# The first expert's low weight halves all on VectorE, its list joins and flags later, w_out's low products last

## The chip, the cores and the metric

The kernel runs on one core of one Trainium2 chip. The metric is the device time of one execution in microseconds (us), smaller being better. Beside the timed runs there is one profiled execution, from which the trace comes. Engines are called TensorE (PE in the rows), VectorE (DVE), ScalarE (ACT), GpSimd (POOL) and SyncE (SP, which here issues most of the DMA transfers); PEld is TensorE's weight load.

## The reference

Attention with a local band and a few global keys, then a dense feed-forward layer, then a top-1 mixture of eight experts. Cut to what matters:

```python
x = attention(q, k, v)                  # 2 x 8 heads x 768 x 64 -> x: 1536 x 512
h = x @ w_in                            # 512 x 2048
x = (h / (1 + exp(-h))) @ w_out         # 2048 x 512
logits = x @ w_gate                     # 512 x 8
e_idx = argmax(logits, axis=1)
gate_w = softmax(logits)[arange(N), e_idx]
eom = sigmoid(x @ w_output_gate)        # 512 x 8
for e in range(8):
    mask = e_idx == e
    ye = maximum(x[mask] @ w1[e], 0) @ w2[e]      # 512 x 1024, 1024 x 512
    out[mask] = gate_w[mask, None] * eom[mask, e, None] * ye
```

## The kernel before

**High and low halves.** A float32 product is made as three products of a rounded format (fp32r): every operand is split into a high half (a rounding copy) and a low half (the operand less its high half), and high x high, high x low and low x high are summed in PSUM. The high half is a copy on ScalarE, the low half a subtraction on VectorE or GpSimd that needs the high half first.

**Stages.** Attention runs over twelve blocks of 128 tokens. The feed-forward layer runs over five groups of 256-token pairs, the first of two pairs and the others of one (`CH`), and each group over 16 slices of the hidden dimension (`f`, called steps 0 to 15 here). In a step TensorE makes the 12 products of `w_in` for slice `f` (`s1_mm`, L315), ScalarE and VectorE evict them in four instructions (L319, L320, L323, L324), and TensorE makes the `w_out` products of slice `f-2` (`s2_mm`, L330 to L332): six per pair, for each of two 128-token halves high x high, low x high and high x low. `w_out`'s low halves are made during the first group and kept in DRAM (`wlo_d`); in later groups SyncE loads them again, four buffers (`wolr`). The evicted slices have six buffers (`g`).

**The first expert, early.** After the last but one group the most used expert so far is known (`order(0)`). In the last ten steps (6 to 15) of the last group, `moe2_pre(k)` loads that expert's weights as 16 quarters of 128 x 512 (`load_u`, SyncE, eight staging buffers `qr`) and splits them (`split_u`, L480 high on ScalarE, L481 low). Steps 8 to 15 split 2, 2, 2, 3, 3, 1, 1 and 2 quarters. In `split_u`, `pool=None` puts the low half of odd `i` on GpSimd and that of even `i` on VectorE. GpSimd also gathers the first rows of that expert (`early_load`, L494) and splits two of the three row blocks (L517). After the last `w_out` product the first 128 rows go through the first expert (`early1` to `early4`).

**The experts.** `order(1)` sorts the experts by use. `load_i(p)` loads two lists of places for expert p (L580), `min_i(p)` joins them by a minimum on VectorE (L584), and `load_x` gathers rows by the joined list (L587, GpSimd). `flags()` is eleven small VectorE instructions whose result is read once, after the last expert. The pass over expert p has eight steps `f`: `f1_mm` (w1 products), `f1_ev` (its eviction, two VectorE and two ScalarE instructions where the window is under 256 rows, as for the first expert), the splits of the next expert's quarters (0, 0, 3, 3, 3, 3, 2, 2 of them in steps 0 to 7; in each step one comes between the two halves of the eviction, and every fourth low half is GpSimd's), `prep_x` (transposes of the next expert's gathered rows) in one step per 128 rows, and `f2_mm` of two steps earlier. The w1 products alternate between two PSUM banks, so step 2 needs step 0's eviction.

**What sets the order.** The program is scheduled by hand: every engine runs its instructions in the order in which the code issues them. An instruction that waits holds up all that stands behind it on its engine, and so it is on SyncE's and GpSimd's DMA queues.

Of the kernel before, what the change touches and what calls it, by code (L numbers as in the profile page):

```python
# [10 lines left out]
F32 = mybir.dt.float32  # L11
# [8 lines left out]
P = 128  # L20
# [3 lines left out]
def kernel(ctx, tc, qk, v, n_global, n_local, w_in, w_out, wg, w1, w2, out):  # L24
# [3 lines left out]
    CH=[[0,1],[2],[3],[4],[5]]  # L28
# [35 lines left out]
    woh={}  # L64
# [256 lines left out]
    def s1_sp(u_,f):  # L321
        t=s1p.pop((u_,f)); g=mp.tile([P,2,256],F32R,tag="g",name="g",bufs=6); gg[u_,f]=g
        A.activation(out=g[:,0],in_=t,func=AF.Copy)  # L323
        V.tensor_tensor(out=g[:,1],in0=t,in1=g[:,0],op=ALU.subtract)  # L324
    def s2_mm(c,u,f):
        if f==0: s2p[u]=[ps.tile([P,512],F32,tag=f"s2{2*(u if c==0 else 0)+k}",name=f"s2{k}",bufs=1) for k in range(2)]
        g=gg.pop((u,f)); wl=wol[c,f]; wh=woh[f//2][:,f%2]
        for k in range(2):
            sl=slice(k*P,(k+1)*P)
            T.matmul(s2p[u][k],g[:,0,sl],wh,start=(f==0),stop=False)  # L330
            T.matmul(s2p[u][k],g[:,1,sl],wh,start=False,stop=False)  # L331
            T.matmul(s2p[u][k],g[:,0,sl],wl,start=False,stop=(f==FB-1))  # L332
    def s2_ev(u):
        xr=mp.tile([P,2,XW],F32,tag="stage",name="xr",bufs=2)
        for k in range(2):
# [236 lines left out]
    def tiles(p):  # L572

        return [(j,min(P,WIN[p]-j*P)) for j in range(R0[p]//P,(WIN[p]+P-1)//P)]
# [7 lines left out]
    def min_i(p):  # L582
        t=ixt[p]; nt=(WIN[p]+P-1)//P
        V.tensor_tensor(out=t[:,0,:nt],in0=t[:,0,:nt],in1=t[:,1,:nt],op=ALU.min)  # L584
# [55 lines left out]
    def moe2_pre(k):  # L640

        q=[(q,i) for q in (0,2,1,3) for i in range(KC)]
        w=(0,0,2,2,2,3,3,1,1,2)
        if 6<=k<16:
            for _ in range(w[k-6]): split_u(*q[nq[1]]); nq[1]+=1
            while nq[0]<min(16,nq[1]+4*(k-5),nq[1]+NQR): load_u(*q[nq[0]]); nq[0]+=1
        if k==6: early_iota()
        if k==7: early_load()
        if k==8: early_rows()
        if k==13: early_prep()  # L650
    def moe2():
        late_split()
        early1(0,0)
        run_gates(2)
        early1(0,1)
        logits(NTT-2)
        early1(1,0)
        run_gates(1)
        late1()
        run_gates(1)  # L660
        early1(1,1)
        early2(0)
        late3()
        order(1)
        moe2_open2()
        load_i(0); load_i(1)
        early3(0,0)
        early2(1)
        early3(0,1); min_i(0); min_i(1); early3(1,0)
        for p in (1,0):  # L670
            for j,n in tiles(p): load_x(p,j)
        early3(1,1)
        flags()
        early4()
        atags[0]=['a','pv','s23']
        LG=2
        steps=[(p,f) for p in range(NE) for f in range(8)]
        for g in range(len(steps)+LG):
            if g<len(steps):
                p,f=steps[g]  # L680
                def spl():
                    split_u(4*(p+1)+nq[1]//4,nq[1]%4,nq[1]%4==1); nq[1]+=1
                f1_mm(p,f)
                if p+1<NE and f==0: nq[:]=[0,0]
                ns=(0,0,3,3,3,3,2,2)[f] if p+1<NE else 0
                f1_ev(p,f,spl if ns else lambda: None)
                if p+1<NE:
                    for _ in range(ns-1): spl()
                    while nq[0]<min(16,nq[1]+4*(f+1),nq[1]+NQR): load_u(4*(p+1)+nq[0]//4,nq[0]%4); nq[0]+=1
                    if p and f==0:  # L690
                        for j,n in tiles(p+1): load_x(p+1,j)
                    if p==0 and f==5:
                        for j,n in tiles(0): fac_x(0,j)
                    if f==2 and p+2<NE: load_i(p+2)
                    if f==5 and p+2<NE: min_i(p+2)
                    t=tiles(p+1)
                    px=PX if p else 3
                    if px<=f<px+len(t): prep_x(p+1,t[f-px][0])
            if g>=LG:
                p2,f2=steps[g-LG]  # L700
                if p2<NE-1:
                    f2_mm(p2,f2)
                    if f2==7: f2_ev(p2)
                elif f2<LASTF:
                    f2_mm(p2,f2)
                elif f2==7:
                    for r in tiles(p2):
                        for k in range(LASTF,8): f2_mm(p2,k,[r])
                        f2_ev(p2,[r])
# [224 lines left out]
    with tc.manual_schedule():  # L934
# [23 lines left out]
        for g in range(len(steps)+LAG):  # L958
# [21 lines left out]
                if g>=LAG+FB: run_gates(2 if g==(len(CH)-1)*FB+2 else 1)  # L980
            if g>=LAG:
                c2,f2=steps[g-LAG]
                for u in CH[c2]:
                    s2_mm(c2,u,f2)
                if f2==FB-1:
                    for u in CH[c2]: gq.append(lambda u=u: s2_ev(u))
                    if c2==0: gq.append(lambda: atags.__setitem__(0,['a','s22','s23']))
                    for u in CH[c2]:
                        for n in (2*u,2*u+1): gq.append(lambda n=n: gate1(n))
                        for fn in (gate2,gate3): gq.append(lambda u=u,fn=fn: fn(u))  # L990
                    run_gates(3 if c2==0 else 1)
                    if c2==len(CH)-2: gq.append(lambda: order(0))
                    if c2==len(CH)-2: gq.append(moe2_open)
# [48 lines left out]
```

## Time and profile before

| | |
|---|---|
| median of 3 runs | 650.11 us (647.69 to 650.35) |
| the profiled execution | 648.54 us |
| its span | 646.8 us |
| TensorE busy | 597.0 us (92%) |
| VectorE busy | 387.3 us (60%) |
| ScalarE busy | 303.4 us (47%) |
| GpSimd busy | 218.0 us (34%) |
| TensorE, 1152 products of w_in (L315) | 154.6 us |
| VectorE, 81 low halves of expert weights (L481) | 75.4 us, 948 ns each on the mean |
| GpSimd, 31 such halves | 40.2 us, 1309 ns each |

Times in the trace count from the span's start. An engine that stands idle costs time only where the chain of work that ends last passes through it; in this kernel that chain lies on TensorE for 78% of the span. Products are pipelined, so a row's duration is longer than the distance to the next row, and the distance is what counts.

### The profile page before, as it was taken

The page shows a single profiled execution, that of the slowest core. Times are in us where ns is not written, and L with a number is a line of the kernel's source. Part 1 is how long each engine was busy: PE and PEld are TensorE (multiplying, and loading weights), DVE is VectorE, ACT ScalarE, POOL GpSimd, SP SyncE. Part 2 cuts the span into 40 slices and gives each one's busy share as a digit, 9 for nine tenths or more (in the row PEclk, how much of TensorE's full clock was granted, in tenths as well). Part 3 has the DMA queues.
Part 4 walks back from the last instruction along what each step waited for, and adds up shares of the span by engine and source line. Part 5 has one row for each costly group of instructions (what it writes and reads, how often), then busy time and mean ns, then how long its engine had stood idle before and what let it go on. Part 6 is the DMA issues. An engine that isn't in the chain of part 4 may idle for free.

```text
span 646.8 us, 12049 instructions
## 1 busy us (share of the span) xinstructions
PE 597.0 (92%) x4054; PEld 506.2 (78%) x4054; DVE 387.3 (60%) x1052; ACT 303.4 (47%) x802; POOL 218.0 (34%) x256
## 2 busy tenths in 40 slices
PE   1898999999997799999999999796999999999994
PEld 1566788888886678888889999685888888888783
DVE  3677589999453545645453344743845479778840
ACT  5577434344442334343432335441745556676741
POOL 3466524444231242222221002731452334443311
PEclk9999999999998999999999999798999999999998
DMA  7144607664347887396447349605957377577500
GB/s 252 41 131 149 225 6 221 221 220 136 121 106 78 131 159 181 98 154 163 124 95 135 83 86 248 201 20 118 295 184 217 111 265 232 185 245 262 171 17 19
DMA packets 83673, 98.77 MB, mean 153 GB/s; under 512 B 35547, under 2 KB 49883, under 8 KB 83602
## 3 DMA queue, kind: packets, MB, share of 16 engines
q1 hardware_dynamic: 76850, 86.69, 49.3%
q0 software_dynamic: 3312, 8.08, 3.8%
q10 hardware_dynamic: 3440, 3.15, 1.6%
q8 instruction: 34, 0.56, 0.4%
q14 instruction: 37, 0.30, 0.2%
HBM read 81.85 MB, written 11.52 MB: 144 GB/s over the span
## 4 chain that ended last, share of the span: by engine, by line
PE 78%; issue 7%; DMA 6%; DVE 5%; ACT 3%; POOL 1%; SPq 0%; POOLq 0%; DVEq 0%; ACTq 0%
PE s L315 20%; PE s L330 7%; PE s L331 6%; PE s L332 6%; PE h L607 5%; PE y L630 4%; PE tp L193 4%; PE y L631 4%; PE h L613 4%; PE y L632 4%; PE qkp L150 3%; PE h L608 3%; DMA vraw<-in_v_dram 3%; PE gl L375 2%; PE px L208 2%
## 5 line engine op out<-in xcount | busy, mean ns | idle before, releaser
L315 PEld LDWEIGHTS s<-xT,wi 128*128 128x128 f32 x1152 | 149.8, 194 | 17.6 <-DVE g L324 9.9
L315 PE MATMUL s<-xT,wi 128*128 128x256 f32 x1152 | 154.6, 287 | 5.4 <-DVE g L324 3.4
L320 DVE SCALAR_TENSOR_TENSOR s<-u,s 128x256 f32<-128x256 f32 x96 | 39.7, 426 | 88.0 <-ACT u L319 87.8
L319 ACT ACTIVATE u<-s 128x256 f32<-128x256 f32 x96 | 35.1, 380 | 115.0 <-PE s L315 114.4
L330 PE MATMUL s<-woh,g 128*128 128x512 f32 x192 | 80.9, 421 | 0.0
L481 DVE TENSOR_TENSOR uq<-qr,uq 128x512 fp32r<-128x512 f32 x81 | 75.4, 948 | 7.7 <-ACT uq L480 4.7
L331 PE MATMUL s<-woh,g 128*128 128x512 f32 x192 | 76.7, 399 | 0.0
L480 ACT ACTIVATE uq<-qr 128x512 fp32r<-128x512 f32 x112 | 66.6, 626 | 8.0 <-DMA qr<-in_w_dram 8.0
L324 DVE TENSOR_TENSOR g<-s,g 128x256 fp32r<-128x256 f32 x96 | 39.3, 422 | 39.6 <-ACT g L323 36.5
L481 POOL TENSOR_TENSOR uq<-qr,uq 128x512 fp32r<-128x512 f32 x31 | 40.2, 1309 | 55.8 <-ACT uq L480 55.7
L630 PE MATMUL y<-uq,hh 128*128 128x512 f32 (+6 forms) x136 | 55.7, 410 | 0.0
L323 ACT ACTIVATE g<-s 128x256 fp32r<-128x256 f32 x96 | 35.6, 379 | 42.8 <-DVE s L320 42.8
L631 PE MATMUL y<-uq,hh 128*128 128x512 f32 (+6 forms) x136 | 53.9, 397 | 0.0
L632 PE MATMUL y<-uq,hh 128*128 128x512 f32 (+6 forms) x136 | 53.7, 395 | 0.0
L332 PE MATMUL s<-wolr,g 128*128 128x512 f32 x128 | 51.7, 404 | 1.0 <-DMA wolr<-wlo_d 1.0
L169 ACT ACTIVATE t<-t,mx 128x256 f32<-128x256 f32 (+1 forms) x96 | 45.8, 480 | 6.5 <-DVE mx L162 4.7
L150 PE MATMUL qkp<-ring 64*128 64x256 f32 (+1 forms) x192 | 34.8, 442 | 13.2 <-DMA ring<-in_qk_dram 12.7
L622 ACT ACTIVATE hh<-h 128x224 fp32r<-128x224 f32 (+6 forms) x64 | 23.3, 363 | 50.3 <-DVE h L620 30.4
L623 DVE SCALAR_TENSOR_TENSOR hh<-h,hh 128x224 fp32r<-128x224 f32 (+6 forms) x64 | 25.2, 395 | 32.0 <-ACT hh L622 32.0
L330 PEld LDWEIGHTS s<-woh,g 128*128 128x128 f32 x192 | 37.1, 193 | 7.4 <-ACT u L319 2.0
L411 POOL DMA_INDIRECT ix<-tok,gdi x12 | 12.4, 1031 | 86.5 <-DVE gsm L415 42.1
L331 PEld LDWEIGHTS s<-woh,g 128*128 128x128 f32 x192 | 37.2, 194 | 4.9
(217 smaller groups left out, 1103.9 us busy)
## 6 DMA issues: line engine op xcount, KB each, us to landing
qr<-in_w_dram SPq DMA_DIRECT2D x128, 256.0 KB, 4.2
wolr<-wlo_d SPq DMA_DIRECT2D x64, 256.0 KB, 3.6
wiraw<-in_w_in_dram SPq DMA_DIRECT2D x16, 512.0 KB, 4.9
wraw<-in_w_out_dram SPq DMA_DIRECT2D x13, 512.0 KB, 3.6
wlo_d<-wol SPq DMA_DIRECT2D x16, 256.0 KB, 2.2
xs<-xr SPq DMA_DIRECT2D x6, 513.0 KB, 8.1
ring<-in_qk_dram SPq DMA_DIRECT2D x12, 256.0 KB, 3.6
ring<-in_qk_dram ACTq DMA_DIRECT2D x10, 256.0 KB, 3.1
```

The costliest lines, as they stand in the source:

```text
L150: T.matmul(q[:,sl],w[:,z,1],w[:,z:z+1,0] if i==0 else w[:,0:3:2,0] if z==0 else w[:,z-1:z+1,0],start=True,stop=True)
L169: A.activation(out=t[:,j,:ce],in_=t[:,j,:ce],func=AF.Exp,scale=0.125,bias=mx[n][:,h:h+1],accum_out=ss[n][:,h:h+1])
L315: T.matmul(t,w[:,ww,kc,:],x[:,xx,kc,:],start=(k==0),stop=(k==11)); k+=1
L320: V.scalar_tensor_tensor(out=t,in0=u,scalar=1.0,in1=t,op0=ALU.add,op1=ALU.mult)
L330: T.matmul(s2p[u][k],g[:,0,sl],wh,start=(f==0),stop=False)
L331: T.matmul(s2p[u][k],g[:,1,sl],wh,start=False,stop=False)
L332: T.matmul(s2p[u][k],g[:,0,sl],wl,start=False,stop=(f==FB-1))
L480: A.activation(out=t[:,0],in_=r,func=AF.Copy)
L481: (G if (i%2 if pool is None else pool) else V).tensor_tensor(out=t[:,1],in0=r,in1=t[:,0],op=ALU.subtract)
L630: T.matmul(o,g[:,0,sl],w[:,0],start=(f==0),stop=False)
L631: T.matmul(o,g[:,1,sl],w[:,0],start=False,stop=False)
L632: T.matmul(o,g[:,0,sl],w[:,1],start=False,stop=(f==7))
```

## The change

Four things move. (1) `moe2_pre` passes `pool=False`: all 16 low halves of the first expert's weights are VectorE's. (2) `min_i` and `load_x` of expert 1 come after step 1 of the first expert's pass and those of expert 0 after its step 2, instead of ahead of the pass; `flags()` stands between the products and the eviction of its step 4, and `early4`, with its output scatter, comes ahead of the gathers. (3) `prep_x` for expert 1 begins at step 4 of the pass instead of step 3. (4) In `s2_mm` the high x low products come after all others of the slice, over both pairs in the first group.

```diff
-    def s2_mm(c,u,f):
-        if f==0: s2p[u]=[ps.tile([P,512],F32,tag=f"s2{2*(u if c==0 else 0)+k}",name=f"s2{k}",bufs=1) for k in range(2)]
-        g=gg.pop((u,f)); wl=wol[c,f]; wh=woh[f//2][:,f%2]
-        for k in range(2):
-            sl=slice(k*P,(k+1)*P)
-            T.matmul(s2p[u][k],g[:,0,sl],wh,start=(f==0),stop=False)
-            T.matmul(s2p[u][k],g[:,1,sl],wh,start=False,stop=False)
-            T.matmul(s2p[u][k],g[:,0,sl],wl,start=False,stop=(f==FB-1))
+    def s2_mm(c,f):
+        if f==0:
+            for u in CH[c]: s2p[u]=[ps.tile([P,512],F32,tag=f"s2{2*(u if c==0 else 0)+k}",name=f"s2{k}",bufs=1) for k in range(2)]
+        g={u:gg.pop((u,f)) for u in CH[c]}
+        wl=wol[c,f]; wh=woh[f//2][:,f%2]
+        for m in range(2):
+            for u in CH[c]:
+                for k in range(2):
+                    sl=slice(k*P,(k+1)*P); o=s2p[u][k]
+                    if m==0:
+                        T.matmul(o,g[u][:,0,sl],wh,start=(f==0),stop=False)
+                        T.matmul(o,g[u][:,1,sl],wh,start=False,stop=False)
+                    else: T.matmul(o,g[u][:,0,sl],wl,start=False,stop=(f==FB-1))
...
-            for _ in range(w[k-6]): split_u(*q[nq[1]]); nq[1]+=1
+            for _ in range(w[k-6]): split_u(*q[nq[1]],pool=False); nq[1]+=1
...
-        early3(0,1); min_i(0); min_i(1); early3(1,0)
-        for p in (1,0):
-            for j,n in tiles(p): load_x(p,j)
+        early3(0,1); early3(1,0)
         early3(1,1)
-        flags()
         early4()
...
                 if p+1<NE and f==0: nq[:]=[0,0]
+                if g==4: flags()
                 ns=(0,0,3,3,3,3,2,2)[f] if p+1<NE else 0
                 f1_ev(p,f,spl if ns else lambda: None)
+                if g in (1,2):
+                    min_i(2-g)
+                    for j,n in tiles(2-g): load_x(2-g,j)
...
-                    px=PX if p else 3
+                    px=PX
...
-                for u in CH[c2]:
-                    s2_mm(c2,u,f2)
+                s2_mm(c2,f2)
```

What this does to VectorE's order shows at two places. The first is steps 11 and 12 of the last feed-forward group, where L320 and L324 are the two evictions of a step and L481 (L486 in the changed file) the low half of a quarter. Before:

```order
L320 SCALAR_TENSOR_TENSOR s_4929<-u,s_4929 128x256
L324 TENSOR_TENSOR g<-s_4929,g 128x256
L481 TENSOR_TENSOR uq<-qr,uq 128x512 x2
L320 SCALAR_TENSOR_TENSOR s_4969<-u,s_4969 128x256
L324 TENSOR_TENSOR g<-s_4969,g 128x256
L481 TENSOR_TENSOR uq<-qr,uq 128x512
L320 SCALAR_TENSOR_TENSOR s_5005<-u,s_5005 128x256
```

Now, at the same place on VectorE:

```order
L320 SCALAR_TENSOR_TENSOR s_4929<-u,s_4929 128x256
L324 TENSOR_TENSOR g<-s_4929,g 128x256
L486 TENSOR_TENSOR uq<-qr,uq 128x512 x3
L320 SCALAR_TENSOR_TENSOR s_4969<-u,s_4969 128x256
L324 TENSOR_TENSOR g<-s_4969,g 128x256
L486 TENSOR_TENSOR uq<-qr,uq 128x512 x3
L320 SCALAR_TENSOR_TENSOR s_5005<-u,s_5005 128x256
```

One half has come to step 11 and two to step 12; they stand ahead of the next step's eviction.

The second place is the start of the first expert's pass on VectorE, where `ixt` is a list of places, `cntf` belongs to the flags, and `h` and `hh` to the eviction of a w1 step. Before, the last low half of the early rows is followed by the joins and the flags:

```order
L557 TENSOR_TENSOR eg<-em,eg 128x512
L584 TENSOR_TENSOR ixt<-ixt 128x3 x2
L443 TENSOR_TENSOR cntf<-cntf,capk 128x8
L444 TENSOR_SCALAR cntf<-pf 128x1
L445 TENSOR_SCALAR cntf<-pf 128x1
```

and the end of the flags, before, by the evictions of steps 0 and 1 on VectorE:

```order
L453 CAST flag<-s_flag 128x1
L620 TENSOR_TENSOR h_5373<-h_5373,hs 128x224
L623 SCALAR_TENSOR_TENSOR hh<-h_5373,hh 128x224
L620 TENSOR_TENSOR h_5396<-h_5396,hs 128x224
L623 SCALAR_TENSOR_TENSOR hh<-h_5396,hh 128x224
```

Now, from the same low half on:

```order
L562 TENSOR_TENSOR eg<-em,eg 128x512
L625 TENSOR_TENSOR h_5340<-h_5340,hs 128x224
L628 SCALAR_TENSOR_TENSOR hh<-h_5340,hh 128x224
L625 TENSOR_TENSOR h_5363<-h_5363,hs 128x224
L628 SCALAR_TENSOR_TENSOR hh<-h_5363,hh 128x224
L589 TENSOR_TENSOR ixt<-ixt 128x3
L625 TENSOR_TENSOR h_5399<-h_5399,hs 128x224
L486 TENSOR_TENSOR uq<-qr,uq 128x512
L628 SCALAR_TENSOR_TENSOR hh<-h_5399,hh 128x224
L589 TENSOR_TENSOR ixt<-ixt 128x3
```

The evictions of steps 0 and 1 stand first, the join for expert 1 is between those of steps 1 and 2, the join for expert 0 behind that of step 2, and the flags are no longer among these rows.

## Rows read from the trace of the kernel before

**Rows 1.** Windows: us; busy PE, PEld, DVE, ACT, POOL (instructions); granted clock; DMA share; GB/s

```profile
385.00:420.00 35.00, 30.57 (x184) 27.04 (x183) 22.15 (x38) 16.19 (x37) 15.93 (x16) 0.91 0.82 224
...
428.00:455.00 27.00, 22.10 (x125) 18.97 (x125) 10.91 (x51) 7.55 (x18) 7.07 (x7) 0.87 0.42 115
455.00:470.00 15.00, 15.00 (x87) 12.99 (x86) 12.42 (x28) 10.64 (x26) 6.17 (x6) 1.00 0.89 278
```

**Rows 2.** Timeline of TensorE, last group's steps 12 to 15: start, us, [idle before]

```profile
402.29 1.59 PE L315 MATMUL s<-xT,wi 128*128 128x256 f32 x12
...
405.11 1.59 PE L315 MATMUL s<-xT,wi 128*128 128x256 f32 x12
406.54 0.40 PE L330 MATMUL s<-woh,g 128*128 128x512 f32 x1
...
409.81 0.40 PE L330 MATMUL s<-woh,g 128*128 128x512 f32 x1
...
411.43 0.50 PE L332 MATMUL s<-wolr,g 128*128 128x512 f32 x1 [0.99 <-DMA wolr<-wlo_d]
...
416.05 2.93 PE L315 MATMUL s<-xT,wi 128*128 128x256 f32 x12 [3.44 <-DVE g L324]
...
423.82 1.54 PE L548 MATMUL eh<-qb,exT 128*128 128x512 f32 x6
```

**Rows 3.** VectorE: low halves 388 to 480 us (ns min/median/max), the long one, an eviction

```profile
L481 DVE TENSOR_TENSOR uq<-qr,uq x18: 675/693/7525, 400.8 to 471.2; 128x512 fp32r<-128x512 f32 x18
...
407.26 7.53 DVE L481 TENSOR_TENSOR uq<-qr,uq 128x512 fp32r<-128x512 f32 x1 [0.61 <-ACT uq L480]
...
L324 DVE TENSOR_TENSOR g<-s,g 128x256 fp32r<-128x256 f32 x96 | 39.3, 422 | 39.6 <-ACT g L323 36.5
```

**Rows 4.** Timeline of GpSimd, the same stretch

```profile
406.74 2.55 POOL L481 TENSOR_TENSOR qb<-qr,qb 128x512 fp32r<-128x512 f32 x2
409.26 4.97 POOL L481 TENSOR_TENSOR uq<-qr,uq 128x512 fp32r<-128x512 f32 x4
```

**Rows 5.** SyncE, the same stretch: two loads, and what they waited for

```profile
401.97 6.43 SPq L475 DMA_DIRECT2D qr<-in_w_dram  x2
...
SPq L475 <- POOL qb L481: 5.5, 1, 5.5
```

**Rows 6.** Timeline of TensorE, first expert's pass, steps 2, 3, 6 and 7

```profile
450.14 1.86 PE L607 MATMUL h<-xw,qb 128*128 128x448 f32 x4 [4.90 <-DVE hh L623]
...
455.03 0.97 PE L607 MATMUL h<-xw,qb 128*128 128x448 f32 x4
...
464.25 0.97 PE L607 MATMUL h<-xw,uq 128*128 128x448 f32 x4
...
466.89 0.97 PE L607 MATMUL h<-xw,uq 128*128 128x448 f32 x4
```

**Rows 7.** Timeline of VectorE, start of that pass

```profile
445.97 0.16 DVE L584 TENSOR_TENSOR ixt<-ixt 128x3 int32<-128x3 int32 x1 [6.12 <-DMA ixt<-ix]
447.70 0.16 DVE L584 TENSOR_TENSOR ixt<-ixt 128x3 int32<-128x3 int32 x1 [1.57 <-DMA ixt<-ix]
...
448.89 0.39 DVE L620 TENSOR_TENSOR h<-h,hs 128x224 f32<-128x224 f32 x1
449.70 0.39 DVE L623 SCALAR_TENSOR_TENSOR hh<-h,hh 128x224 fp32r<-128x224 f32 x1 [0.42 <-ACT hh L622]
```

**Rows 8.** That pass: first gather, landing of gathers; first quarter load, median landing of quarters

```profile
448.82 1.04 POOL L587 DMA_INDIRECT xw<-xs,ixt  x1 [12.82 <-DMA qr<-in_w_dram]
...
DMA to landing us min/median/max: 4.6/5.3/6.7
...
445.89 0.35 SPq L475 DMA_DIRECT2D qr<-in_w_dram  x1
...
qr<-in_w_dram SPq DMA_DIRECT2D x24, 256.0 KB, 4.4
```

**Rows 9.** End of the first group: ScalarE's evictions, TensorE's transposes

```profile
173.43 2.07 ACT L336 ACTIVATE xr<-s 128x512 f32<-128x512 f32 x4 [0.39 <-DMA xs<-zx]
...
176.21 0.66 PE L367 MATMUL gt<-ident,xr 128*128 128x128 f32 x4
```

## The prediction, made before the changed kernel was run

> **What bounds the kernel now.** I read the stretches first, then TensorE's rows, then whoever its waits name. TensorE is busy nearly throughout, so only stretches where it is not can give much. Two of them can: 385 to 420 us, with 30.57 of 35 us busy and a mean granted clock of 0.91, and 428 to 455 us, with 22.10 of 27 us and 0.87 [rows 1]. The first is the end of the feed-forward's last group, the second the start of the experts. The longest wait on VectorE, 4.9 us, is in the second [rows 6].
>
> In the first, a step of the last group is 12 products of w_in (405.11 to 406.54, 1.43 us) and six of w_out; a whole step takes 2.82 us (402.29 to 405.11), so the six take 1.39. Step 14 runs as usual until TensorE waits 0.99 us for a low half of w_out coming back by DMA, and then 3.44 us for VectorE before step 15 [rows 2]. When it starts again at 416.05 it does so at the lower of its two clock levels (1.2 of 2.4 GHz): the 12 products take 2.7 us to 418.8 where 1.43 was usual.
>
> VectorE is late because of one instruction. The low half of an expert weight quarter takes 693 ns at the median and 7525 at the longest [rows 3]; the long one begins at 407.26. All that time GpSimd runs the halves dealt to it: two from 406.74, four from 409.26, ending at 414.23 [rows 4], without a gap, since they had piled up behind its early gathers. VectorE's half ends at 414.79, 0.56 us after the last of them. So one VectorE half stood still while GpSimd worked, and behind it stood the two evictions that TensorE needed. The same pile keeps staging buffers occupied: SyncE's two quarter loads from 401.97 take 6.43 us [rows 5], 5.5 of them waiting for the first of GpSimd's halves, and a w_out low half stands behind them in its queue. That is the 0.99 us.
>
> In the second stretch TensorE finishes two w1 steps of the first expert and then waits for VectorE until 450.14 [rows 6]. VectorE has two joins of lists of places in its queue, waiting for DMA 6.12 and 1.57 us, then the flags, 447.86 to 448.89, 1.0 us, and only then the eviction of step 0 [rows 7]. The step from 450.14 to 455.03 takes 4.89 us at the low clock; the one from 464.25 to 466.89 takes 2.64.
>
> **First edit: all 16 first-expert halves on VectorE.** Eight halves leave GpSimd. On VectorE eight more at 0.69 us each add 5.5 us at most; since consecutive ones start about 0.1 us before the last has ended, 4.9 is my working figure. In 385 to 420 us VectorE shows 22.15 us busy, of which 6.8 are the standstill (7.53 less 0.69), so it would hold some 15.3 + 4.9 = 20.2 us of 35 [rows 1, 3]. Cover is thinnest in steps 11 and 12, now three halves each: with two evictions of 0.42 us [rows 3] that is 2.6 to 2.9 us in a step of 2.82. TensorE needs an eviction only two steps later, so a small overrun there is absorbed, and later steps have one or two halves.
>
> What is removed: step 14's six products go on at 409.81 without a wait and end at 411.20; 12 products and the last 18 follow: 411.20 + 1.43 + 3 x 1.39 = 416.80. The next work, the first expert's first product, started at 423.82 [rows 2]. That is **7.0 us**: 4.85 of waiting (416.05 less 411.20) and 2.17 of the low clock. What is late next? The quarters: SyncE no longer stands at 401.97, so they and the w_out low halves are issued up to 5.5 us earlier. GpSimd keeps the two halves of the early gathered rows, moved forward, and can hold a VectorE half for 2.5 us, but in steps 13 and 14 there is one half each. I let both ends stand: 5.0 if these show by 2 us, 7.2 if smaller stalls fall too.
>
> The Trainium skill ("SBUF — State Buffer", Who interferes with whom) says that a VectorE instruction with two SBUF inputs contends with a GpSimd one that reads SBUF, and that the later of the two is shut out until the other's instruction is over. By that rule the long half would have gone on when the GpSimd half then running ended, by 409.3 at the latest, and at the early rows a VectorE half would be held for one half instead of two, which would put my lower end at about 6 instead of 5.0. The trace has it held through all six halves [rows 3, 4], so the lower end stays.
>
> **Second edit: joins after the second and third w1 product, flags at the fifth step.** The joins (0.16 us each) and gathers change place, no instruction is saved. All times here are on the old axis; the list loads follow the gate, which moves with TensorE. Step 0's eviction now comes first. Its two VectorE instructions and ScalarE's between took 448.89 to 450.09, 1.20 us [rows 7]; started at about 444.5, when step 0's products are done and ScalarE has copied from them, they end at 445.7, and step 2 starts near 445.8 instead of 450.14: 4.34 us. It then runs at the full clock, 2.64 for 4.89: 2.25 more. Together 6.6 [rows 6].
>
> Against it stand two new waits. The first expert-1 join still ends at about 447.9, but the reader of its gathered rows comes earlier. Step 4's transposes are reached at 445.8 + 2 x 2.64 + 1.25 = 452.3 (a step less its six products, 2.64 - 1.39, is 1.25), moved one step later by the edit or they would stand at 449.7. The first gather started 448.82 and gathers land 4.6 to 6.7 us after issue, 5.3 at the median [rows 8]. Issue between 447.9 and 448.8 gives landings of 452.5 to 455.5, a wait of 0.2 to 3.2; I take 1.5, near the median landing. Also expert 1's quarters: their first load goes out at 445.89 and lands 4.4 later at the median, 450.3 [rows 8], and a ScalarE copy of it stands ahead of step 2's eviction. That may hold step 4 by some 0.7 us, inside the same wait. Second, VectorE: busy 12.42 of 15 us in 455 to 470 [rows 1], it must now do this work sooner with the flags' 1.0 us among it; I take 0.4, bounds 0 and 1.0. The output scatter of the early rows goes ahead of the gathers in GpSimd's queue, at a time when GpSimd was waiting for lists anyway. The flag is only read at the end. So 6.6 - 1.5 - 0.4 = **4.7 us**, from 2.4 to 6.4.
>
> **Third edit: w_out's low products last.** Same products, each with the same stationary load; 0 us. A low half may now come 0.46 us later in a one-pair group, but the only wait it had goes with the first edit. In the first group, with two pairs, a pair's first sum is complete at the ninth product of twelve, not the third, 1.4 us later; its evictions began at 173.43 and the transposes that read them at 176.21 without a wait [rows 9], so 0.3 us of delay at the start is covered. The g buffers of the first pair are free four products later, but two more products and 12 of w_in still lie before the next writer: 1.9 us.
>
> **Sum.** 7.0 + 4.7 + 0 = 11.7 us. The profiled execution took 648.54 us (span 646.8 and 1.7 around it): 636.8. It is 1.6 below the median of the three runs and 0.6 below the mean of all four; I add 0.6: **637.4 us**.
>
> **Rivals.**
> A. The first pass waits for its rows. If gathers land late, step 4 waits 3.2 us and its clock falls again, costing another 2.25: 6.6 - 3.2 - 2.25 - 0.4 = 0.75 for the second edit, 7.75 in all, 641.4 us. For it: the 6.7 us landing and a DMA system full of quarters; against: TensorE had no wait there before.
> B. The eight halves come out on TensorE. 4.9 us of the 7.0 are given back: 6.8 in all, 642.4 us. For it: steps 11 and 12 are full; against: two steps of slack.
> The Trainium skill ("Perfetto Trace Analysis", Optimizing Scalar/DVE Operations) suggests moving work off a saturated VectorE, even to GpSimd, adding that between these two it may not help because they share an SBUF port. The first half of that speaks for B; the 7.5 us half speaks for the second half.
> C. Slower: B, and TensorE's clock follows. If VectorE's steps 11 and 12 pass 2.82 us and the delay is not absorbed, TensorE waits in every step from 10 on and runs at 1.2 GHz: six steps at 5.64 instead of 2.82 cost 16.9, plus the 4.9: 7.0 - 21.8 + 4.7 = -10.1, so 659.2 us. It decides when a step's VectorE work exceeds the step by more than the two-step slack; the low clock did follow the one long stall. Against: only two steps come near.
> D. The second edit does nothing: a list lands later than now, so that the join, now ahead of step 2's eviction, stalls as before. 7.0 alone: 642.1 us. B and D together: 2.1, 647.1 us, no change that shows.
>
> **How the numbers follow.** Forecast 0.65, A 0.15, B 0.07, D 0.04, B with D 0.05, C 0.04. A measurement of this kernel can tell about 0.5%, 3.3 us, from no change. Faster by more: forecast, A, B and D, 0.91; within it 0.05; slower 0.04. The forecast's own ends are 5.0 + 2.4 = 7.4 and 7.2 + 6.4 = 13.6, that is 635.5 to 641.7, and runs lie up to 2.7 us from each other; with A and B the range is 633.5 to 642.5.
>
> **What would show it.** Right: no VectorE half over about 2 us between 395 and 425; no TensorE wait before step 15; the first expert's first product near 417; after its second w1 product a gap of under 1 us, not 4.9; no stretch at 1.2 GHz in either place; then a wait of 1 to 2 us at step 4's transposes, released by a gather. Wrong: TensorE waiting for VectorE in steps 11 to 15, or at step 2 with a join still in front.

## The result, and the profile after

The changed kernel takes 640.72 us at the median of four runs (637.42 to 643.52), the kernel before beside it 648.9 us (four runs, 644.24 to 650.35). The ratio is 0.9876, with an interval of 0.9841 to 0.9911: 8.0 us faster (0.0124 of 648.9; gains below are worked out in the same way), somewhere from 5.8 to 10.3. The forecast was 637.4 us, 11.7 us less than the profiled execution of before.

The profiled execution of the changed kernel took 643.52 us, the longest of its four, with a span of 641.8 us: 5.0 us less than the span of before. The stretches after, in the columns of [rows 1]:

```profile
385.00:420.00 35.00, 32.21 (x193) 28.61 (x192) 20.50 (x47) 16.91 (x41) 8.16 (x10) 0.95 0.91 224
428.00:455.00 27.00, 23.81 (x147) 20.46 (x147) 14.68 (x46) 10.68 (x24) 10.11 (x10) 1.00 0.52 149
455.00:470.00 15.00, 14.33 (x84) 12.36 (x83) 11.65 (x37) 8.63 (x21) 5.54 (x5) 1.00 0.92 297
```

In the second stretch the granted clock went from 0.87 to 1.00, in the first only from 0.91 to 0.95, and TensorE is still 2.8 us short of 35 there. The first place is clear from VectorE's halves, in the view of [rows 3], 388 to 480 us:

```profile
L486 DVE TENSOR_TENSOR uq<-qr,uq x25: 676/687/958, 405.6 to 478.3; 128x512 fp32r<-128x512 f32 x25
```

The half of 7525 ns is gone; the longest here takes 958. So the cause that the prediction named was removed. TensorE's timeline of the last group, beginning with steps 9 and 10, shows what came instead:

```profile
394.33 1.59 PE L315 MATMUL s<-xT,wi 128*128 128x256 f32 x12
397.15 1.59 PE L315 MATMUL s<-xT,wi 128*128 128x256 f32 x12
402.93 1.73 PE L315 MATMUL s<-xT,wi 128*128 128x256 f32 x12 [2.79 <-DVE g L324]
407.01 1.97 PE L315 MATMUL s<-xT,wi 128*128 128x256 f32 x12
410.20 1.59 PE L315 MATMUL s<-xT,wi 128*128 128x256 f32 x12
...
421.87 1.56 PE L553 MATMUL eh<-qb,exT 128*128 128x512 f32 x6
```

The two waits of [rows 2] at steps 14 and 15 are gone, but step 11 now waits 2.79 us for an eviction of step 9, and the step that it begins takes 4.08 us (402.93 to 407.01) instead of 2.82, with a granted clock of 0.86 from 403 to 405 us and of 0.52 from 405 to 408. The first expert's first product comes at 421.87, not near 417. Why the eviction is late stands in ScalarE's timeline and in VectorE's:

```profile
398.24 0.63 ACT L485 ACTIVATE qb<-qr 128x512 fp32r<-128x512 f32 x1 [3.78 <-DMA qr<-in_w_dram]
399.68 0.63 ACT L485 ACTIVATE qb<-qr 128x512 fp32r<-128x512 f32 x1 [0.81 <-DMA qr<-in_w_dram]
400.22 0.36 ACT L319 ACTIVATE u<-s 128x256 f32<-128x256 f32 x1
```

```profile
401.57 0.42 DVE L320 SCALAR_TENSOR_TENSOR s<-u,s 128x256 f32<-128x256 f32 x1
402.44 0.42 DVE L324 TENSOR_TENSOR g<-s,g 128x256 fp32r<-128x256 f32 x1 [0.45 <-ACT g L323]
```

ScalarE's copies of the first two quarters stand ahead of step 9's eviction (L319), and they wait for the quarters. In the chain of waits (start, duration, what) that transfer is one piece:

```profile
390.84 8.82 DMA qr<-in_w_dram
```

8.8 us, where [rows 8] has 4.4 at the median for quarters. So the new wait is called VectorE's, but it is a DMA's, two engines away.

At the second place, TensorE's timeline of the first expert's pass, steps 2 to 4:

```profile
443.85 1.08 PE L612 MATMUL h<-xw,qb 128*128 128x448 f32 x4 [0.56 <-DVE hh L628]
...
446.60 0.97 PE L612 MATMUL h<-xw,qb 128*128 128x448 f32 x4
...
449.24 0.98 PE L612 MATMUL h<-xw,uq 128*128 128x448 f32 x4
...
453.29 0.66 PE L600 MATMUL xm<-ident,xw 128*128 128x128 f32 x4 [2.63 <-DMA xw<-xs,ixt]
...
464.81 1.94 PE L618 MATMUL h<-xwT,uq 128*128 128x304 f32 x12 [0.67 <-ACT xwT L602]
```

The 4.90 us of [rows 6] have become 0.56, and the step from 443.85 takes 2.75 us instead of 4.89. Step 4's transposes wait 2.63 us for the gathered rows, and the end of the pass 0.67. On VectorE the join and the flags, and on GpSimd the first gather and the pair of weight halves:

```profile
445.71 0.16 DVE L589 TENSOR_TENSOR ixt<-ixt 128x3 int32<-128x3 int32 x1 [0.78 <-DMA ixt<-ix]
...
452.79 2.90 DVE L448 TENSOR_TENSOR cntf<-cntf,capk 128x8 f32<-128x8 f32 x1
...
456.64 0.39 DVE L625 TENSOR_TENSOR h<-h,hs 128x224 f32<-128x224 f32 x1
```

```profile
446.75 1.04 POOL L592 DMA_INDIRECT xw<-xs,ixt  x1 [3.94 <-DMA qr<-in_w_dram]
...
453.11 2.54 POOL L486 TENSOR_TENSOR uq<-qr,uq 128x512 fp32r<-128x512 f32 x2
```

The join waits 0.78 us behind the eviction, where it costs nothing. The first flags instruction, 128 x 8 numbers, takes 2.90 us beside GpSimd's pair, so that step 4's eviction begins only at 456.64.

For the experiments two distances on TensorE are used, the same in every kernel: **A**, from step 8's first w_in product in the last group to the first expert's first product, and **B**, from the first w1 product of the first expert's pass to that of the second expert's pass. Before, A was 32.85 us and B 26.95; after, 30.36 and 24.19. What lies between A and B takes 18.7 to 18.8 us in every profile. The forecast was 25.85 for A and 22.25 for B.

### The profile page after: what moved, and what is told of

It is laid out like the page before. It is cut to its first block, busy times and chain, and to the rows that moved or that the text cites. A ratio compares the mean times of both kernels' runs of the same rounds, so it can differ in the third digit from the quotient of the medians.

```text
span 641.8 us, 12050 instructions
## 1 busy us (share of the span) xinstructions
PE 594.5 (93%) x4054; PEld 504.1 (79%) x4054; DVE 387.0 (60%) x1060; ACT 303.1 (47%) x802; POOL 207.9 (32%) x248
## 4 chain that ended last, share of the span: by engine, by line
PE 65%; DVE 11%; DMA 8%; issue 7%; ACT 5%; POOL 2%; SPq 1%; POOLq 0%; DVEq 0%; ACTq 0%
PE s L315 15%; PE s L335 5%; PE s L336 5%; PE s L337 5%; PE h L612 4%; PE h L618 4%; PE tp L193 4%; PE y L635 3%; PE y L637 3%; PE y L636 3%; PE qkp L150 3%; DMA qr<-in_w_dram 3%; DMA vraw<-in_v_dram 3%; PE h L613 2%; PE gl L380 2%
## 5 line engine op out<-in xcount | busy, mean ns | idle before, releaser
L320 DVE SCALAR_TENSOR_TENSOR s<-u,s 128x256 f32<-128x256 f32 x96 | 39.7, 426 | 84.1 <-ACT u L319 82.4
L319 ACT ACTIVATE u<-s 128x256 f32<-128x256 f32 x96 | 35.2, 380 | 114.3 <-PE s L315 113.6
L486 DVE TENSOR_TENSOR uq<-qr,uq 128x512 fp32r<-128x512 f32 x87 | 71.3, 840 | 10.6 <-ACT uq L485 7.8
L324 DVE TENSOR_TENSOR g<-s,g 128x256 fp32r<-128x256 f32 x96 | 39.2, 422 | 39.8 <-ACT g L323 37.2
L486 POOL TENSOR_TENSOR uq<-qr,uq 128x512 fp32r<-128x512 f32 x25 | 33.0, 1330 | 52.8 <-ACT uq L485 52.8
L337 PE MATMUL s<-wolr,g 128*128 128x512 f32 x128 | 41.2, 404 | 0.0
L187 POOL TENSOR_SCALAR dg<-ident,ss 128x128 f32<-128x128 f32 x48 | 28.4, 602 | 33.6 <-DVE ss L185 17.3
```

What stands on the lines that cost most here:

```text
L320: V.scalar_tensor_tensor(out=t,in0=u,scalar=1.0,in1=t,op0=ALU.add,op1=ALU.mult)
L337: else: T.matmul(o,g[u][:,0,sl],wl,start=False,stop=(f==FB-1))
L486: (G if (i%2 if pool is None else pool) else V).tensor_tensor(out=t[:,1],in0=r,in1=t[:,0],op=ALU.subtract)
```

## The experiments

Kernels that ran on the same chip share the runs of the kernel before, and those of one chip are given together. "Theory" in the texts is the prediction with what the first profile had added to it.

### The three edits one by one

On this chip the kernel before took 654.08 us (35 runs, 649.84 to 659.68).

**First edit alone**, on the kernel before:

```diff
-            for _ in range(w[k-6]): split_u(*q[nq[1]]); nq[1]+=1
+            for _ in range(w[k-6]): split_u(*q[nq[1]],pool=False); nq[1]+=1
```

> The kernel before with the first edit alone: all 16 first-expert halves on VectorE. The theory (one VectorE half stood still for 7.5 us behind GpSimd's six) expects no VectorE half over 2 us, and 2 to 7 us less time in all, 7 where nothing else stalls the last group and about 2.5 where TensorE waits again for late quarters as it did in the profile of the changed kernel; the 4.9 us wait in the first expert's pass stays. Rival B (the eight halves come out on TensorE) expects 2 us or less, with waits for VectorE in steps 11 and 12.

Measured: 650.05 us, ratio 0.9943 [0.9912, 0.9974], 3.7 us less. A is 30.46 us and B 27.35. TensorE's waits of its profile from 390 to 450 us:

```profile
395.03 0.50 PE L332 MATMUL s<-wolr,g 128*128 128x512 f32 x1 [0.35 <-DMA wolr<-wlo_d]
...
412.62 0.63 PE L509 MATMUL em<-ident,ex 128*128 128x128 f32 x4 [2.00 <-DMA ex<-xs,ei]
...
449.40 1.86 PE L607 MATMUL h<-xw,qb 128*128 128x448 f32 x4 [4.89 <-DVE hh L623]
```

The two waits of [rows 2], for VectorE before step 15 and 0.99 us for a low half of w_out, have gone here too; a wait of 0.35 us for such a half stands in step 8. In this run no late quarter held TensorE; instead the early gathered rows (`ex`) came 2.00 us after their transposes were reached. The 4.89 us in the pass belong to the second edit and stay.

**Second edit alone** (the joins, gathers and flags later, the transposes a step later, on the kernel before):

```diff
-        early3(0,1); min_i(0); min_i(1); early3(1,0)
-        for p in (1,0):
-            for j,n in tiles(p): load_x(p,j)
+        early3(0,1); early3(1,0)
...
+                if g==4: flags()
...
+                if g in (1,2):
+                    min_i(2-g)
+                    for j,n in tiles(2-g): load_x(2-g,j)
```

> The kernel before with the second edit alone: joins, gathers, flags and the transposes one step later. The theory expects the wait of 4.9 us before step 2 of the first expert's pass to fall under 1 us, a new wait of 1.5 to 3 us for gathered rows at step 4, and 2.5 to 5 us less time; the 7.5 us VectorE half stays. Rival D (the edit does nothing) expects the wait before step 2 to stay and no change in time.

Measured: 651.51 us, ratio 0.9946 [0.9914, 0.9977], 3.5 us less. A is 33.63 us and B 26.02:

```profile
417.99 2.93 PE L315 MATMUL s<-xT,wi 128*128 128x256 f32 x12 [4.05 <-DVE g L324]
...
451.29 1.08 PE L607 MATMUL h<-xw,qb 128*128 128x448 f32 x4 [0.57 <-DVE hh L623]
...
461.88 1.11 PE L595 MATMUL xm<-ident,xw 128*128 128x128 f32 x4 [3.41 <-DMA xw<-xs,ixt]
```

The first row is the old standstill, untouched by this edit: a VectorE half takes 5.93 us here. The second is the wait of [rows 6] without the joins; the third is the price, 3.41 us, somewhat above the 1.5 to 3 us of the text.

**Third edit alone** (`s2_mm` of the changed kernel in the kernel before):

```diff
+        for m in range(2):
+            for u in CH[c]:
+                for k in range(2):
...
+                    else: T.matmul(o,g[u][:,0,sl],wl,start=False,stop=(f==FB-1))
```

> The kernel before with the third edit alone: the low products of w_out last. The theory expects no change, within 1 us, and the one wait for a low half of w_out (0.99 us) shorter by up to 0.5 us. A rival that says the order itself costs expects TensorE's step in the first group over 5.64 us, or a wait for g.

Measured: 654.18 us, ratio 0.9998 [0.9967, 1.0029], A 36.02 us and B 27.82. No change in the time that can be told; the profiled execution is the longest of its 12 (657.58 us). The wait of 0.99 us for `wolr` does not occur in its profile, but the one for VectorE does, and one more that makes A as long as it is:

```profile
407.62 2.47 PE L315 MATMUL s<-xT,wi 128*128 128x256 f32 x12 [2.78 <-DVE g L324]
...
424.69 2.48 PE L315 MATMUL s<-xT,wi 128*128 128x256 f32 x12 [3.56 <-DVE g L324]
```

The first of these is step 11 behind late first quarters, as in the changed kernel, though the halves are dealt out as before. So this wait is not made by the first edit. It can occur in either kernel.

**The whole change once more:**

> The changed kernel once more, as a second profile. The profile had TensorE wait 2.8 us before step 11 of the last group, since the first quarters landed 8 us after issue instead of 5. If that is chance, differing between executions, this profile shows the wait elsewhere or not at all and a span of 636 to 640 us; if the change causes it, the same wait of 2 to 3 us stands there again.

Measured: 649.08 us, ratio 0.9907 [0.9871, 0.9943], 6.1 us less. A is 31.68 us and B 26.64, with 3.71 us of waiting at step 11 and 3.77 at the gather. The parts alone make 3.7 + 3.5 + 0.1 = 7.3 us, which agrees with 6.1 within the intervals. So nothing shows that one edit eats what another gives; with intervals of 2 us to either side, a loss of 1 or 2 us would not show.

### What makes the first quarters late

Two suspects: full DMA queues, or something that slows them. The windows of the changed kernel's trace for two microseconds each (columns as in [rows 1]) speak for the second:

```profile
388.00:390.00 2.00, 2.00 (x15) 1.87 (x14) 0.83 (x2) 0.38 (x1) 0.77 (x1) 1.00 1.53 64
390.00:392.00 2.00, 2.00 (x14) 1.74 (x13) 0.75 (x2) 0.77 (x2) 1.70 (x4) 1.00 1.02 169
392.00:394.00 2.00, 2.00 (x15) 1.83 (x14) 0.48 (x2) 0.39 (x1) 0.00 (x0) 1.00 0.94 327
394.00:396.00 2.00, 2.00 (x17) 1.88 (x16) 0.47 (x2) 0.38 (x1) 0.00 (x0) 1.00 1.59 115
396.00:398.00 2.00, 2.00 (x14) 1.78 (x13) 0.00 (x0) 0.00 (x0) 0.00 (x0) 1.00 0.92 42
```

From 394 to 398 us the DMA engines are as busy as ever (1.59 and 0.92 in the last column but one, which adds up the time of all packets and so can pass 1) and move 115 and 42 GB/s, where 392 to 394 us had 327 with 0.94. The same is seen at 388. Ahead of each such stretch GpSimd's timeline has a scatter of the fourth group's token numbers into the lists of places, in 4-byte elements:

```profile
384.04 0.99 POOL L416 DMA_INDIRECT ix<-tok,gdi  x1 [39.76 <-DVE gsm L420]
389.23 0.97 POOL L416 DMA_INDIRECT ix<-tok,gdi  x1 [4.19 <-DMA ix<-tok,gdi]
```

To test it, the two scatters of the fourth group of tokens were left out, so that the rows of these tokens are missing from the output:

```diff
-        for t in range(2):
+        for t in range(0 if u==4 else 2):
```

> The changed kernel without the two scatters of the fourth group's token numbers into the lists of places (its tokens are left out of every list, so their output rows are not written). In both profiles of the changed kernel single 2 KB packets of other transfers took 1 to 3 us, not the usual 0.08, some 2 to 5 us after each of these scatters of 4-byte elements, and the first quarters landed late. If the scatters cause it, the slow packets between 386 and 404 us go, the first quarter is used about 5 us after its issue, and TensorE has no wait for VectorE before step 11. If the store of the group's rows or chance causes it, slow packets stay there.

Measured: 645.12 us (one run), where the kernel before took 655.81 us on this chip (seven runs). A is 26.57 us, 0.7 above the 25.85 forecast for the first edit. There is no wait ahead of step 11, and the windows are clean:

```profile
386.00:388.00 2.00, 2.00 (x14) 1.78 (x13) 1.38 (x7) 0.56 (x3) 0.00 (x0) 1.00 0.11 41
388.00:390.00 2.00, 2.00 (x13) 1.71 (x12) 0.98 (x5) 0.96 (x3) 0.00 (x0) 1.00 0.15 55
390.00:392.00 2.00, 2.00 (x16) 1.89 (x15) 1.44 (x8) 0.32 (x2) 0.00 (x0) 1.00 1.01 282
...
394.00:396.00 2.00, 2.00 (x14) 1.74 (x12) 0.61 (x2) 0.77 (x2) 0.00 (x0) 1.00 0.58 160
396.00:398.00 2.00, 2.00 (x15) 1.84 (x14) 0.48 (x2) 0.39 (x1) 0.00 (x0) 1.00 0.96 341
```

With scatters, 64 GB/s cost a share of 1.53; without, 55 cost 0.15.

One run alone would not settle it, since late quarters come and go with the scatters in place. The other profiles do. In each of the 13 with these scatters, 38 to 93 packets of 2 KB that began between 383 and 410 us took over 1 us; without them five did, none before 407 us.

And what is late goes with the distance of the two scatters. In seven profiles GpSimd starts the second 5.2 to 6.1 us after the first: the three of the changed kernel, the third edit alone, and three of the kernels below (four halves on GpSimd, the splits a step later, the halves in the changed kernel's steps). There the first quarters are late, and TensorE waits 2.1 to 4.3 us at step 11 in all but the one with the splits a step later. In the other six the distance is 9.0 to 9.9 us, and none has that wait. So the scatters make the quarters late. What sets their distance, and what in a scatter slows the rest, was not found out. The wait at the gather stayed, 3.69 us, with B at 25.99: these two scatters do not make it.

### How long a half is held

The prediction said that a VectorE half stands still for all that GpSimd has in a row, not for one instruction. Here four of the kernel's eight halves of the first expert stay on GpSimd:

```diff
-            for _ in range(w[k-6]): split_u(*q[nq[1]]); nq[1]+=1
+            for _ in range(w[k-6]): split_u(*q[nq[1]],pool=q[nq[1]][1]==1); nq[1]+=1
```

> The kernel before with four of the eight halves left on GpSimd and four moved to VectorE. Three of the four are ready when the early gathers let GpSimd go, and run without a gap. If a VectorE half is held until the whole queue of GpSimd halves is through, one VectorE half takes 3 to 4.5 us. If it is held for one instruction of GpSimd's, none takes over 2 us.

Measured: 649.98 us (one run); A 31.64, B 27.11. GpSimd's timeline, VectorE's, and VectorE's halves from 405 to 420 us:

```profile
412.59 1.30 POOL L481 TENSOR_TENSOR qb<-qr,qb 128x512 fp32r<-128x512 f32 x1
413.85 2.52 POOL L481 TENSOR_TENSOR uq<-qr,uq 128x512 fp32r<-128x512 f32 x2
```

```profile
413.41 4.12 DVE L481 TENSOR_TENSOR uq<-qr,uq 128x512 fp32r<-128x512 f32 x2 [0.61 <-ACT uq L480]
```

```profile
L481 DVE TENSOR_TENSOR uq<-qr,uq x7: 680/691/3524, 407.5 to 418.8; 128x512 fp32r<-128x512 f32 x7
```

One of the two halves in VectorE's row takes 3.52 us. If it is the first, which the rows don't tell apart, it began in the first of GpSimd's three (412.59 to 413.89) and ended 0.56 us after the last of them (416.93 and 416.37), as the long one of before did. The same is seen with the second edit alone, where GpSimd has four halves in a row from 411.17 to 416.16 us and VectorE's half takes 5.93 us, to 416.72, again 0.56 us later. Six in a row held it for 7.53 us, four for 5.9, three for 3.5: the length follows GpSimd's row of work. A also holds 2.34 us of waiting at step 11, behind late first quarters.

### Giving the two late transfers room

On the same chip as the two before (the kernel before at 655.81), **the splits one step later**:

```diff
-        w=(0,0,2,2,2,3,3,1,1,2)
+        w=(0,0,0,2,2,2,3,3,2,2)
```

> The changed kernel with the splits of the first expert's quarters one step later (0, 2, 2, 2, 3, 3, 2, 2 in steps 8 to 15, not 2, 2, 2, 3, 3, 1, 1, 2). If late first quarters held ScalarE and so the evictions, the wait of 2.8 to 3.7 us before step 11 falls under 1 us and the time falls by 2 to 4 us against the changed kernel. If VectorE's load holds TensorE, the wait moves to steps 13 to 15 and nothing is gained.

Measured: 646.49 us, ratio 0.9855 [0.9802, 0.9908]; A 30.84, B 26.84. The wait at step 11 has gone, though the first quarters were late here too (ScalarE's copies wait 1.27 and 1.19 us for them), and others stand in its place, for transfers and not for VectorE, so that A is as long as in the changed kernel. That kernel was not run on this chip, so the 2 to 4 us of the text can't be read off:

```profile
404.00 0.74 PE L337 MATMUL s<-wolr,g 128*128 128x512 f32 x2 [1.04 <-DMA wolr<-wlo_d]
407.62 0.73 PE L337 MATMUL s<-wolr,g 128*128 128x512 f32 x2 [0.52 <-DMA wolr<-wlo_d]
413.25 0.63 PE L514 MATMUL em<-ident,ex 128*128 128x128 f32 x4 [2.08 <-DMA ex<-xs,ei]
```

**The second expert's transposes behind the step's w2 products**, so that the gathered rows may come six products later:

```diff
-                    if px<=f<px+len(t): prep_x(p+1,t[f-px][0])
+                    if p and px<=f<px+len(t): prep_x(p+1,t[f-px][0])
...
+                if p2==0 and 2<=f2<5: prep_x(1,tiles(1)[f2-2][0])
```

> The changed kernel with the transposes of expert 1's gathered rows behind the step's w2 products, not ahead of them, in the first expert's pass. The gathers land when they land, so the wait at step 4 (2.6 and 3.8 us in two profiles) should fall by the six products' 1.4 us and the time by 1 to 1.5 us against the changed kernel. If VectorE holds the pass instead, a wait for VectorE appears in steps 5 to 7 or at the next expert's first step, and less is gained.

Measured: 646.74 us, ratio 0.9894 [0.9829, 0.9958]; A 29.87, B 24.94. The wait at the gather is 2.45 us in its profile, against 2.63 to 3.77 in the kernels with the transposes ahead of the products: less, but not the 1.4 us less of the six products. Waits of 0.44 us for VectorE in step 7 and of 0.79 us for ScalarE at the second expert's first product have come, as the text's second reading has it in part.

On a third chip (the kernel before at 654.37 us, 23 runs) **the change once more, to compare with**:

> The changed kernel once more, as the kernel beside which the other three of this chip are read. Both theories: 5 to 8 us below the kernel before; TensorE waits 2 to 4 us in the last group, at step 11 or at the early rows' transposes, and 2 to 4 us at the first pass's step 4 for a gather.

Measured: 648.98 us (12 runs, 646.22 to 651.98), ratio 0.9919 [0.9888, 0.9951]; A 32.15 with 4.29 us of waiting at step 11, B 25.51 with 3.19 at the gather.

**All of this room together**, with the early rows' transposes a step later and the flags at step 20:

```diff
-        w=(0,0,2,2,2,3,3,1,1,2)
+        w=(0,0,0,2,2,2,3,3,2,2)
...
-        if k==13: early_prep()
+        if k==14: early_prep()
...
-                if g==4: flags()
+                if g==20: flags()
...
+                if p2==0 and 2<=f2<5: prep_x(1,tiles(1)[f2-2][0])
```

> The changed kernel with the halves one step later, the early rows' transposes one step later (14 instead of 13), expert 1's transposes behind the second products, and the flags at step 20. Theory (what is left of the two losses are two late DMAs, the first quarters and the gathers, and can be given room): no wait over 1 us at the early rows and under 1 us at the first pass's gather, 2 to 4 us below the changed kernel. Rival (the waits only change place, because VectorE then is too full at the end of the last group): within 1 us of the changed kernel, with a wait for a VectorE half at the first expert's first products.

Measured: 645.83 us (six runs, 641.92 to 646.93), ratio 0.9862 [0.9813, 0.9911]; A 27.73, the shortest with all the work in place, and B 24.71. TensorE does not wait between step 8 and the end of step 15 of the last group; what is left is 1.21 us behind the last step, for ScalarE:

```profile
419.63 0.50 PE L335 MATMUL s<-woh,g 128*128 128x512 f32 x1 [1.21 <-ACT g L323]
...
453.38 0.66 PE L600 MATMUL xm<-ident,xw 128*128 128x128 f32 x4 [1.82 <-DMA xw<-xs,ixt]
```

The theory held for the early rows and for the time, not for the gather, which is still waited for 1.82 us where under 1 was expected; behind it come 0.71 us for VectorE and 0.99 us for ScalarE. In that pass three GpSimd halves in a row from 454.12 us hold one of VectorE's for 5.04 us. Four of the six runs lie below the fastest of the changed kernel's 12 on this chip. The two intervals overlap, but the six and the 12 runs beside each other have means of 645.1 and 649.3 us, 4.2 us apart (2.0 to 6.3 by their spread), so the gain is clear of noise. That step 11 has no wait in this profile says nothing of the later splits, since the two scatters lie 9.8 us apart in it; for these the splits-later kernel above speaks. Four things were moved here at once, and which of them gives how much was not separated.

**The same with the halves in the changed kernel's steps:**

> As the one before, but with the halves in the steps of the changed kernel. Theory: step 11 waits 2 to 4 us for late first quarters as in the changed kernel, the early rows and the first pass's gather hardly wait: 1 to 3 us below the changed kernel, and slower than the kernel with the halves one step later by 1 to 2 us. Rival (the first quarters' wait is made good because the early rows then are there in time): as fast as the one with the halves later.

Measured: 646.88 us (12 runs), ratio 0.9886 [0.9846, 0.9925]; A 29.87 with 2.08 us at step 11, B 24.65 with 1.72 at the gather. It lies between the other two, as the theory said, but the intervals of all three overlap, and the gather was waited for more than "hardly"; 1.59 us for ScalarE at the second expert's first product follow.

**The flags alone later:**

```diff
-                if g==4: flags()
+                if g==20: flags()
```

> The changed kernel with the flags at step 20 instead of step 4. Theory (the 2.9 us for which VectorE is held at step 4 are covered, since TensorE waits for the gather anyway): within 0.5 us of the changed kernel. Rival (the held VectorE sets when the pass goes on): 1 to 2 us faster, and the wait at the gather goes with it.

Measured: 646.69 us (six runs, 645.29 to 655.21), ratio 0.9899 [0.984, 0.9958] without the run at 655.21: not to be told from the changed kernel, so that the time does not choose between the two texts. A is 28.20 in its profile. The gather was waited for all the same, 3.23 us, as the theory has it. But both texts took it that the standstill would go with the flags, and it did not: VectorE's next weight half is the one held, 3.10 us beside the same pair on GpSimd:

```profile
454.33 3.10 DVE L486 TENSOR_TENSOR uq<-qr,uq 128x512 fp32r<-128x512 f32 x1 [0.86 <-ACT uq L485]
```

Behind the wait for the gather, which ends at 453.79, the clock fell to its lower level, 0.50 from 454 to 457 us in the windows, where 1.00 was granted before it:

```profile
448.00:451.00 3.00, 2.42 (x12) 1.59 (x10) 2.04 (x5) 1.91 (x5) 2.39 (x3) 1.00 0.91 287
451.00:454.00 3.00, 0.21 (x1) 0.22 (x2) 1.99 (x4) 2.37 (x6) 2.39 (x3) 0.76 1.02 392
454.00:457.00 3.00, 3.00 (x10) 2.36 (x10) 2.67 (x1) 1.93 (x5) 2.85 (x3) 0.50 1.05 393
```

B is 26.94, as long as before the change. Step 11 did not wait in this run; GpSimd's second scatter into the lists had started at 395.64, and the first quarters were copied from 397.93. In the changed kernel's first profile it started at 389.23, while the first quarters were on their way.

## Why the prediction was right, and where it was not

**Direction, time and range were right.** 640.72 us lies in 633.5 to 642.5, and the change is faster by more than can be mistaken. But the gain was put at 11.7 us, and three chips measured 8.0, 6.1 and 5.3 us (the last is 0.0081 of 654.37). On the last two, where the kernel before is slower as well (654.08 and 654.37 us), the changed kernel's 649.08 and 648.98 us lie above the range, and the gains lie below the forecast's own lower end of 7.4. So that time and range came out on the first chip is in part luck: each of the two terms, 7.0 and 4.7, was too large. Two of the rivals' sums are off by 0.1 us (B gives 642.3, B with D 647.0), which changes nothing.

**First edit, "7.0 us": mechanism right, term too large.** The half that stood still, the w_out low half behind SyncE's wait, and the low clock at step 15 all went. VectorE is busy 20.50 us in 385 to 420, against "some 20.2", and the first edit alone has no wait for VectorE in the last group: rival B, the eight halves coming out on TensorE, did not happen, and rival C neither. What failed is the sentence "What is late next?". It looked at the quarters after 401.97 and not at the first ones, whose copies stand ahead of step 9's eviction in ScalarE's queue, nor at the early rows. In the six profiles with this stretch as changed TensorE waits each time for one or the other: at step 11 2.79, 3.71 and 4.29 us, or at the early rows' transposes 2.00 us (first edit alone), 2.07 (transposes behind the w2 products) and 1.88 (flags alone later). A is 30.36, 31.68, 32.15, 30.46, 29.87 and 28.20 us in them, 30.5 on the mean, and 32.85, 33.63 and 36.02 without the first edit, 34.2: 3.7 us are gained where 7.0 were forecast, as much as the time of the first edit alone shows. The lower end of 5.0 did not hold it. With the scatters taken away A is 26.57, 6.3 below the 32.85 of before; the kernel before without scatters was not run.

By the prediction's own list, "TensorE waiting for VectorE in steps 11 to 15" would show it wrong, and at step 11 it does; nor did the first expert's first product come near 417 (421.87). The releaser named in the row was the last link of a chain that begins at a DMA.

The Trainium skill ("SBUF — State Buffer", Who interferes with whom) has the later of the two engines shut out until the other's instruction is over. Where the prediction set it against [rows 3, 4], the measurement decides for the rows: three halves in a row held one for 3.5 us, four for 5.9, six for 7.5, and one instruction of GpSimd takes 1.3.

**Second edit: the gain right, a price too small.** 6.6 us were forecast from the join; the profile has 4.34 (4.90 less 0.56) and 2.14 (4.89 less 2.75), 6.5 in all. The end of the pass waits 0.67 us, for ScalarE; 0.4 stood there for VectorE. The wait at the gather was put at 1.5 within 0.2 to 3.2: it is 2.63 in the first profile, and 3.77, 3.19, 3.41, 3.69 and 3.75 in others with the same pass. The landing at the median of [rows 8], 5.3 us, was too short: gathers now land in 5.6 to 6.8 us, 6.2 at the median, while quarters move. So 6.5 - 2.6 - 0.7 = 3.2 us, where 2.8 were gained in B (26.95 to 24.19).

**Rival A is half of the truth.** It said that the first pass waits 3.2 us for its rows and that the clock falls again. In the first profile the clock stayed at 1.00 behind a wait of 2.63 us. Behind the longer waits it did fall: to 0.59 and 0.63 for three microseconds in the two other profiles of the same kernel, to 0.62 with the second edit alone, to 0.50 with the flags later. Over six profiles with the second edit B is 25.9 us on the mean, over four without it 27.3: 1.4 us, between the forecast's 4.7 and rival A's 0.75. Its total, 7.75 us, is nearer to the three measurements than the forecast's.

**Third edit: 0 us, as forecast** (0.1 us faster, interval from 1.9 slower to 2.2 faster).

**What stays open.** The two distances explain 3.7 + 1.4 = 5.1 us on the mean, and the times say 5.3, 6.1 and 8.0. For the second edit alone the time says 3.5 us (1.5 to 5.6) where B has 1.4; the rest was not found. In the first pair of profiles A and B give 2.5 + 2.8 us and the rest of the span -0.3, which makes its 5.0. Across profiles, step 8 of the last group begins anywhere from 390.97 to 395.91 us in kernels that are nearly the same up to there, and that spread is larger than the remainder. Why gathers are late besides their landing time was not settled either.

## What to carry to other kernels

When a stall is taken away, look up for each instruction queued near it what else it needs, and when that arrives: the next latest thing sets the time, and here it was a transfer two engines away from the wait that the profile named. Where an in-order queue mixes evictions that TensorE needs with work on data that is still on its way, put a step of slack between the load and that work; the version that does so for the quarters, the early rows and the gathered rows is the fastest with all its work, 645.83 us beside 648.98 and 654.37, though slack for one of them alone only let the next one show. And a VectorE weight half beside GpSimd's stood still for the whole row that GpSimd had piled up, so pile-ups on GpSimd can matter more than their busy time.

## What was not expected of the hardware

- Behind a scatter of single 4-byte elements, other DMA traffic slowed to 42 to 115 GB/s at a full busy share, for 2 to 4 us: single 2 KB packets took up to 3.1 us in the changed kernel's first profile, where 0.08 is the median. With the scatters left out the slow stretches between 386 and 404 us went, and A was 26.57 us, where the three profiles of the changed kernel have 30.36, 31.68 and 32.15.
- A VectorE instruction on 128 x 8 numbers took 2.90 us beside two GpSimd weight halves of 2.54 us, though its row begins 0.32 us earlier than theirs.
